# Normalised attention and leaky-ReLU MLP in one kernel: an opening in a new order, GpSimd squares behind gates, softmax sums by halves of the queries

## The chip, the cores and the metric

One core of one Trainium2 chip runs the whole program. The metric is the device time of one execution in microseconds; the median of three executions counts. Engine names are those of the profile: PE is TensorE's matmul side and PEld its weight load, DVE is VectorE, ACT is ScalarE, POOL is GpSimd, SP is SyncE.

## The reference

Queries, keys and values have 8 batches, 12 heads, 448 positions and 64 channels. Queries and keys are divided by their root mean square and scaled by a gain, then comes softmax attention, then a two-layer MLP on all heads of a position together (768 to 2048 to 768 channels, leaky ReLU between).

```python
def rmsnorm(x, g):
    rms = np.sqrt(np.mean(x * x, axis=-1, keepdims=True) + 1e-06)
    return x / rms * g
q_n, k_n = (rmsnorm(q, g_q), rmsnorm(k, g_k))
scores = scale * np.matmul(q_n, k_n.transpose(0, 1, 3, 2))
scores = scores - np.max(scores, axis=-1, keepdims=True)
attn = np.exp(scores)
attn = attn / (np.sum(attn, axis=-1, keepdims=True) + 1e-09)
attn_out = np.matmul(attn, v)
x = attn_out.transpose(0, 2, 1, 3).reshape(8 * 448, 768)
h = x @ w_in
out = np.maximum(0.01 * h, h) @ w_out
```

## The kernel before

The work is cut into 24 units of four heads of one batch; three units fill the 768 channels of a batch. A unit's q and k lie as 128 rows by 896 columns each. Per unit:

- squares (`prep_sq` on ACT or `prep_sqp` on GpSimd), their sums (`prep_ssq`, DVE), the inverse root (`prep_rinv`, two ACT instructions), the normalised values in fp16 (`prep_norm`, DVE), and a transposition, in the opening on PE;
- scores for seven groups of keys (`qk`), a shift from the maximum of the first group (`shift_max`, a broadcast by a matmul in `shift_mm`, and a bias `eb`), seven exponentials on ACT (`ex`);
- sums of the exponentials over the keys, by matmuls with ones, the product with v (`pv`), and a multiplication by the inverse sums (`xmul`).

The MLP's matmuls are held in a queue, and from unit 3 on they are dealt out between the steps of the attention. Units 0 to 2 have none of them beside them: this is the opening, written out by hand. `warm` issues matmuls whose results nobody uses. They keep TensorE active while there is no other work for it.

```python
            nc.scalar.activation(buf(u, f"sq{ti}")[:, :, c[0]:c[1]], raw[u][ti][:, :, c[0]:c[1]], AF.Square)

    def prep_sqp(u, tis=BOTH):
        for ti in tis:
            nc.gpsimd.tensor_tensor(buf(u, f"sq{ti}"), raw[u][ti], raw[u][ti], op=ALU.mult)

    def prep_g(u):
        nc.vector.tensor_scalar(buf(u, "qkT")[:, 0], buf(u, "qkT")[:, 0], gcol, None, op0=ALU.mult)

    def prep_ssq(u, c=ALL, tis=BOTH):
        for ti in tis:
            nc.vector.tensor_reduce(buf(u, "ssq")[:, ti, :, c[0]:c[1]], buf(u, f"sq{ti}")[:, :, c[0]:c[1]],
                                    axis=AXL.X, op=ALU.add)

    def prep_rinv(u, tis=BOTH):
        x = slice(tis[0], tis[-1] + 1)
        nc.scalar.activation(buf(u, "uu")[:, x], buf(u, "ssq")[:, x], AF.Ln, bias=eps_t, scale=1.0 / D)
        nc.scalar.activation(buf(u, "rinv")[:, x], buf(u, "uu")[:, x], AF.Exp, bias=0.0, scale=-0.5)

    def prep_norm(u, c=ALL, tis=BOTH):
        n = c[1] - c[0]
        for ti in tis:
            src = raw[u][ti]
            nc.vector.tensor_tensor(
                buf(u, "n16")[:, ti, c[0]:c[1]].rearrange("p s a d -> p a s d"), src[:, :, c[0]:c[1]],
                buf(u, "rinv")[:, ti, :, c[0]:c[1], None].broadcast_to([P, 2, n, D]), op=ALU.mult)

    def prep_tr(u, ti, copies):
        tp = aux([P, NS, P], FP16, "tp")
        for (lo, hi), copy in copies:
            for x in range(lo, hi):
...
    def shift_max(u):
        s = st[u]
        sT = s["sT"][0][1]
        if isinstance(sT, list):
            pm2 = small.tile([P, 2], FP32, tag="pm2", name="pm2")
            for a in range(2):
                nc.vector.tensor_reduce(pm2[:, a:a + 1], sT[a][:, 0:S], axis=AXL.X, op=ALU.max)
            s["spare"] = sT[0]
            nc.vector.tensor_reduce(s["spare"][:, 511:512], pm2, axis=AXL.X, op=ALU.max)
        else:
            s["spare"] = sT[:, 0]
            nc.vector.tensor_reduce(s["spare"][:, 511:512], sT[:, :, 0:S], axis=AXL.XY, op=ALU.max)
        s["dg"] = small.tile([P, P], FP16, tag="dg", name="dg")
        nc.vector.tensor_tensor(s["dg"], ident16, s["spare"][:, 511:512].broadcast_to([P, P]), op=ALU.mult)
...
    def shift_mm(u):
        s = st[u]
...
        else:
            if "pb" not in s:
                shift_bank(u)
            pb = s["pb"]
            nc.tensor.matmul(pb[:, 0:P], onesp, s["dg"], start=True, stop=True)
            nc.vector.tensor_reduce(s["spare"][:, 510:511], pb[:, 0:P], axis=AXL.X, op=ALU.max)
        s["eb"] = small.tile([P, 1], FP32, tag="eb", name="eb")
        nc.vector.tensor_scalar(s["eb"], s["spare"][:, 510:511], -1.0, DELTA, op0=ALU.mult, op1=ALU.add)

    def gate(u):
        nc.gpsimd.tensor_copy(gate_t, buf(u, "n16")[:, 1, NS - 1, 1, D - 1:D])
```

`gate` copies one element of the last normalised values on GpSimd. All that GpSimd does behind it, squares as well as its own transfers, therefore starts only when the normalisation has ended.

The sums for units 4 to 22 (`narrow`) use the column groups of TensorE: even groups of keys go to two of them, odd ones to the other two, and the two halves are added on DVE. Then ACT takes the logarithm and the exponential of its negative, and transfers spread the inverse sums over the rows.

```python
    def zcol(u):
        s = st[u]
        s["zc"] = aux([P, 512], FP32, "zc")
        for t in (0, 1, 6, 2, 3, 4, 5):
            for a in range(2):
                halves = ((t % 2, 0, S),) if t < NS - 1 else ((0, 0, S // 2), (1, S // 2, S))
                for y, lo, hi in halves:
                    c = 32 * (2 * y + a)
                    nc.tensor.matmul(s["zc"][c:c + 32, lo:hi], onesr, s["et"][:, t, a, lo:hi],
                                     start=(t < 2), stop=(t in (4, 5)))
...
    def zcol_sum(u):
        s = st[u]
        s["zs"] = zpool.tile([64, S], FP32, tag="zs", name="zs")
        nc.vector.tensor_copy(s["zs"], s["zc"][64:128, 0:S])
        nc.vector.tensor_tensor(s["zs"], s["zc"][0:64, 0:S], s["zs"], op=ALU.add)

    def zcol_inv(u):
        s = st[u]
        nc.scalar.activation(s["zs"], s["zs"], AF.Ln)
        nc.scalar.activation(s["zs"], s["zs"], AF.Exp, bias=0.0, scale=-1.0)
        s["rz"] = zpool.tile([P, 2, S], FP32, tag="rz", name="rz")
        for r in range(2):
            src = s["zs"][r:64:2, None, :]
            nc.sync.dma_start(s["rz"][:, r], src.broadcast_to([32, 4, S]))
```

The opening:

```python
        load(0)
        load(1)
        load(2)
        gps = aux([P, 512], FP32, "gps")
        wbank = aux([P, 512], FP32, "warm")
        warm(32, wbank)
        for a in range(2):
            nc.vector.scalar_tensor_tensor(gdup[:, a], grow[:, 0], 0.125, grow[:, 1], op0=ALU.mult, op1=ALU.mult)
        nc.tensor.matmul(gps[:, 0:1], gdup.rearrange("o a d -> o (a d)"), one32, start=True, stop=True)
        warm(42, wbank)
        prep_sq(0, CA, (0,))
        prep_sq(0, CB, (0,))
        prep_sq(0, ALL, (1,))
        prep_ssq(0, CA, (0,))
...
        nc.vector.tensor_copy(gcol, gps[:, 0:1])
        prep_ssq(0, ALL, (1,))
        prep_rinv(0, (1,))
        prep_sqp(1, (0,))
        load_v(0)
        load_v(1)
        prep_norm(0, CA, (0,))
        prep_norm(0, CB, (0,))
        prep_tr(0, 0, ((CA, acopy), (CB, acopy)))
        prep_norm(0, K0, (1,))
        tpk = aux([P, NS, P], FP16, "tp")

        def trk(c, copy):
            for x in range(*c):
                nc.tensor.transpose(tpk[:, x, :], buf(0, "n16")[:, 1, x].rearrange("p a d -> p (a d)"), ident16)
            copy(buf(0, "qkT")[:, 1, c[0]:c[1]], tpk[:, c[0]:c[1]])

        trk(K0, vcopy)
        prep_norm(0, K1, (1,))
        qk(0, STEPS[0])
        shift_max(0)
        trk(K1, acopy)
        load(3)
        prep_sqp(1, (1,))
        gate(0)
        load_w_in(0, 1024)
        prep_sqp(2)
        shift_bank(0)
        warm(12, st[0]["pb"])
        shift_mm(0)
        load_v(2)
        prep_ssq(1, ALL, (0,))

        def feed(u):
            load(u + 4)
            gate(u + 1)
            prep_sqp(u + 3)
            load_v(u + 3)
...
        def close(u):
            n = u + 1
            zsum_slot(u)
            ex(n)
            qk(n, (1,))
            pv(u)
            zinv(u)

        ex(0)
        prep_ssq(1, ALL, (1,))
        prep_rinv(1)
        prep_norm(1)
        prep_ssq(2)
        feed(0)
        load_w_in(1024, 1024)
        wb = aux([P, 512], FP32, "warm")
        qk(0, (1,))
        ex(0)
        warm(16, wb)
        qk(0, (2,))
        ex(0)
        warm(12, wb)
        qk(0, (3,))
        ex(0)
        warm(6, wb)
        qk(0, (4,))
        ex(0)
        trn(1, 0, vcopy)
        trn(1, 1, acopy)
        qk(0, (5,))
        ex(0)
        qk(0, (6,))
        ex(0)
        prep_rinv(2)
        score0(1)
        shift_max(1)
        shift_bank(1)
        warm(20, st[1]["pb"])
        shift_mm(1)
        close(0)
        ...
        prep_norm(2)
        prep_ssq(3)
        ex(1)
        feed(1)
        for f in range(2):
            load_w_out(8 * f, 8)
        qk(1, (2,))
```

The steps of a later unit that bear on the sums: `zcol` and `zcol_sum` run at the start of the next unit, `zcol_inv` in its first step, and the multiplication in the second step on GpSimd, or in the third on DVE for three of the units.

Of the kernel before, what the change touches and what calls it, by code (L numbers as in the profile page):

```python
# [18 lines left out]
def kernel(  # L19
# [113 lines left out]
# [3 lines that stand above are left out]
# [124 lines left out]

    def zcol(u):
        s = st[u]
        s["zc"] = aux([P, 512], FP32, "zc")
        for t in (0, 1, 6, 2, 3, 4, 5):
            for a in range(2):
                halves = ((t % 2, 0, S),) if t < NS - 1 else ((0, 0, S // 2), (1, S // 2, S))
                for y, lo, hi in halves:
                    c = 32 * (2 * y + a)
                    nc.tensor.matmul(s["zc"][c:c + 32, lo:hi], onesr, s["et"][:, t, a, lo:hi],  # L269
                                     start=(t < 2), stop=(t in (4, 5)))  # L270
# [12 lines left out]
    def zcol_sum(u):  # L283
        s = st[u]
        s["zs"] = zpool.tile([64, S], FP32, tag="zs", name="zs")
        nc.vector.tensor_copy(s["zs"], s["zc"][64:128, 0:S])
        nc.vector.tensor_tensor(s["zs"], s["zc"][0:64, 0:S], s["zs"], op=ALU.add)

    def zcol_inv(u):
        s = st[u]  # L290
        nc.scalar.activation(s["zs"], s["zs"], AF.Ln)
        nc.scalar.activation(s["zs"], s["zs"], AF.Exp, bias=0.0, scale=-1.0)  # L292
        s["rz"] = zpool.tile([P, 2, S], FP32, tag="rz", name="rz")
        for r in range(2):
            src = s["zs"][r:64:2, None, :]
            nc.sync.dma_start(s["rz"][:, r], src.broadcast_to([32, 4, S]))
# [279 lines left out]
    with tc.manual_schedule():  # L576
# [22 lines left out]
        prep_sqp(1, (0,))  # L599
        load_v(0)  # L600
        load_v(1)
        prep_norm(0, CA, (0,))
        prep_norm(0, CB, (0,))
        prep_tr(0, 0, ((CA, acopy), (CB, acopy)))
        prep_norm(0, K0, (1,))
        tpk = aux([P, NS, P], FP16, "tp")

        def trk(c, copy):
            for x in range(*c):
                nc.tensor.transpose(tpk[:, x, :], buf(0, "n16")[:, 1, x].rearrange("p a d -> p (a d)"), ident16)  # L610
            copy(buf(0, "qkT")[:, 1, c[0]:c[1]], tpk[:, c[0]:c[1]])

        trk(K0, vcopy)
        prep_norm(0, K1, (1,))
        qk(0, STEPS[0])
        shift_max(0)
        trk(K1, acopy)
        load(3)
        prep_sqp(1, (1,))
        gate(0)  # L620
        load_w_in(0, 1024)
        prep_sqp(2)
        shift_bank(0)
        warm(12, st[0]["pb"])
        shift_mm(0)
        load_v(2)
        prep_ssq(1, ALL, (0,))

        def feed(u):
            load(u + 4)  # L630
            gate(u + 1)
            prep_sqp(u + 3)
            load_v(u + 3)

        def trn(u, ti, copy):
            prep_tr(u, ti, ((ALL, copy),))
# [5 lines left out]
        def close(u):  # L642
            n = u + 1
            zsum_slot(u)
            ex(n)
            qk(n, (1,))
            pv(u)
            zinv(u)

        ex(0)  # L650
        prep_ssq(1, ALL, (1,))
        prep_rinv(1)
        prep_norm(1)
        prep_ssq(2)
        feed(0)
        load_w_in(1024, 1024)
        wb = aux([P, 512], FP32, "warm")
        qk(0, (1,))
        ex(0)
        warm(16, wb)  # L660
        qk(0, (2,))
        ex(0)
        warm(12, wb)
        qk(0, (3,))
        ex(0)
        warm(6, wb)
        qk(0, (4,))
        ex(0)
        trn(1, 0, vcopy)
        trn(1, 1, acopy)  # L670
        qk(0, (5,))
        ex(0)
        qk(0, (6,))
        ex(0)
        prep_rinv(2)
# [3 lines left out]
        warm(20, st[1]["pb"])  # L679
        shift_mm(1)  # L680
        close(0)

        prep_norm(2)
        prep_ssq(3)
        ex(1)
        feed(1)
# [13 lines left out]
        prep_rinv(3)  # L700
# [7 lines left out]
        close(1)  # L708

        prep_norm(3)  # L710
        ex(2)
        feed(2)
# [137 lines left out]
```

## Time and profile before

| quantity | value |
|---|---|
| median of three executions | 431.97 us (430.81 to 432.87) |
| profiled execution, span | 429.5 us |
| mean granted TensorE clock | 0.992 |
| unused matmuls (`warm`) | 152 |
| first exponential of unit 0 | starts at 17.67 us |
| first exponential of unit 1 | starts at 28.48 us |
| first exponential of unit 2 | starts at 37.40 us |
| first exponential of unit 3 | starts at 49.60 us |

The profile gives busy time by engine, by stretch of the span, by group of like instructions, and the instructions in order of time. Bracketed entries tell how long the engine was idle ahead of an instruction and what ended that. A busy matmul engine is not necessarily one at its peak, because a matmul's recorded length holds its pipeline as well. A long duration of a DVE or GpSimd instruction need not be work: an engine that has begun an instruction and cannot go on is recorded as busy.

### The profile page before, as it was taken

What the parts mean: (1) busy time and instruction counts of PE and PEld (TensorE: products, weight loads), DVE (VectorE), ACT (ScalarE), POOL (GpSimd) and SP (SyncE); (2) the same over time, 40 slices, a digit from 0 to 9 for tenths busy, and PEclk for the clock granted to TensorE, in tenths of its full rate; (3) what the DMA queues carried; (4) which work ended last, traced back from release to release, by engine and by line L of the source; (5) the groups of instructions that cost most, each with busy time, mean ns of one, the idle gap of its engine ahead of it and who ended that gap; (6) DMA issues with size and microseconds to landing.
All of it is one profiled execution on the core that took longest, in us unless ns stands there. A gap on an engine that the chain in (4) does not pass through costs nothing.

```text
span 429.5 us, 8844 instructions
## 1 busy us (share of the span) xinstructions
PE 409.5 (95%) x3645; PEld 211.3 (49%) x3645; DVE 272.1 (63%) x434; ACT 306.5 (71%) x466; POOL 86.5 (20%) x77
## 2 busy tenths in 40 slices
PE   7677999999999999999999999999999999999996
PEld 6444444444444544455445544455445544455563
DVE  5898656888669865487359864587459840541162
ACT  4389888757986779967986789967986767643400
POOL 3875323300002102111102102111101101110000
PEclk9699999999999999999999999999999999999999
DMA  7999994789666896578665797489582460212013
GB/s 253 196 241 249 240 248 110 120 183 221 168 104 115 190 215 161 140 133 195 170 111 130 188 192 168 134 140 188 169 110 44 118 149 11 44 38 73 2 45 103
DMA packets 66476, 62.37 MB, mean 145 GB/s; under 512 B 35716, under 2 KB 61572, under 8 KB 66436
## 3 DMA queue, kind: packets, MB, share of 16 engines
q1 hardware_dynamic: 55840, 49.62, 47.0%
q0 software_dynamic: 10272, 11.80, 17.9%
q8 instruction: 28, 0.46, 0.4%
q10 hardware_dynamic: 324, 0.39, 0.3%
q14 instruction: 12, 0.10, 0.1%
HBM read 45.61 MB, written 11.01 MB: 132 GB/s over the span
## 4 chain that ended last, share of the span: by engine, by line
PE 64%; ACT 17%; DVE 10%; issue 2%; DMA 1%; SPq 0%; ACTq 0%; DVEq 0%
PE hps L347 23%; ACT et L201 8%; PE md L427 7%; PE mc L427 7%; PE sT L182 6%; PE ma L427 6%; PE sT L326 5%; ACT gt L341 4%; PE op L387 3%; PE zc L269 3%; PE mb L427 2%; DVE n L154 2%; ACT x L281 1%; DVE ssq L142 1%; ACT zs L292 1%
## 5 line engine op out<-in xcount | busy, mean ns | idle before, releaser
L201 ACT ACTIVATE et<-sT,eb 128x896 f16<-128x896 f32 x166 | 158.5, 1004 | 15.6 <-PE sT L182 13.3
L347 PE MATMUL hps<-xt,win 128*128 128x448 f16 x756 | 151.1, 353 | 0.2 <-DVE xt L335 0.2
L347 PEld LDWEIGHTS <-win 128*128 128x128 f16 x756 | 70.6, 98 | 71.5 <-issue 10.1
L341 ACT ACTIVATE gt<-hps 128x448 f16<-128x448 f32 x126 | 65.7, 540 | 19.3 <-PE hps L347 18.7
L306 POOL TENSOR_TENSOR xt<-x,rz 128x896 f16<-128x896 f32 x16 | 33.5, 2091 | 150.1 <-DMA rz<-zs 49.1
L154 DVE TENSOR_TENSOR n<-rq,rinv 128x896 f16<-128x896 f32 (+2 forms) x25 | 29.0, 1164 | 47.8 <-ACT rinv L148 44.3
L182 PE MATMUL sT<-qkT 64*64 64x448 f16 x664 | 52.8, 367 | 4.7 <-ACT et L201 4.2
L142 DVE TENSOR_REDUCE ssq<-sq 128x14 f32<-128x896 f32 (+2 forms) x49 | 50.3, 1055 | 1.3 <-ACT sq L131 1.3
L427 PEld LDWEIGHTS <-sa 128*128 128x128 f16 x352 | 32.8, 98 | 26.3 <-issue 6.1
L281 ACT COPY x<-sT 128x896 f32<-128x896 f32 x19 | 17.2, 906 | 37.8 <-DVE sT L232 37.8
L111 POOL DMA_DIRECT2D vt<-in_v_dram x24 | 18.2, 758 | 112.2 <-PE sT L326 104.8
L219 DVE TENSOR_REDUCE sT<-sT 128x1 f32<-128x896 f32 x22 | 24.0, 1093 | 18.3 <-PE sT L182 18.3
L182 PEld LDWEIGHTS <-qkT 64*64 64x64 f16 x672 | 15.8, 104 | 38.9 <-issue 35.5
L427 PEld LDWEIGHTS <-gt 128*128 128x128 f16 x264 | 25.3, 98 | 19.0 <-issue 2.9
L387 PE MATMUL op<-wout,gt 128*128 128x384 f16 x192 | 34.1, 327 | 0.0
L427 PE MATMUL ma<-wout,gt 128*128 128x384 f16 x176 | 32.3, 326 | 0.4
L154 DVE TENSOR_TENSOR n<-rk,rinv 128x896 f16<-128x896 f32 (+2 forms) x25 | 28.9, 1156 | 0.0
L326 PE MATMUL sT<-et,vt 64*64 64x448 f16 x532 | 28.5, 349 | 0.3
L408 DVE TENSOR_TENSOR sa<-gt 128x512 f16<-128x512 f16 (+1 forms) x15 | 8.1, 542 | 30.3 <-ACT gt L341 30.3
L326 PEld LDWEIGHTS <-vt 64*64 64x64 f16 x672 | 20.4, 107 | 10.8 <-issue 1.1
L387 PEld LDWEIGHTS <-gt 128*128 128x128 f16 x192 | 17.7, 98 | 14.0 <-issue 3.2
L453 ACT COPY ost<-ma 128x384 f32<-128x384 f32 x11 | 5.3, 479 | 23.7 <-PE ma L427 23.7
(87 smaller groups left out, 443.5 us busy)
## 6 DMA issues: line engine op xcount, KB each, us to landing
rq<-in_q_dram SPq DMA_DIRECT2D x24, 448.0 KB, 4.8
rk<-in_k_dram SPq DMA_DIRECT2D x24, 448.0 KB, 5.9
out_dram<-ost SPq DMA_DIRECT2D x52, 192.0 KB, 4.0
rz<-zs SPq DMA_DIRECT2D x38, 224.0 KB, 3.3
vt<-in_v_dram POOLq DMA_DIRECT2D x24, 224.0 KB, 5.0
win<-in_moe_w_in_dram POOLq DMA_DIRECT2D x8, 384.0 KB, 8.9
wout<-in_moe_w_out_dram POOLq DMA_DIRECT2D x2, 1536.0 KB, 23.7
out_dram<-ost SPq DMA_DIRECT2D x4, 96.0 KB, 2.1
```

What stands on the lines that cost most here:

```text
L142: nc.vector.tensor_reduce(buf(u, "ssq")[:, ti, :, c[0]:c[1]], buf(u, f"sq{ti}")[:, :, c[0]:c[1]], axis=AXL.X, op=ALU.add)
L154: nc.vector.tensor_tensor(buf(u, "n16")[:, ti, c[0]:c[1]].rearrange("p s a d -> p a s d"), src[:, :, c[0]:c[1]], buf(u, "rinv")[:, ti, :, ...
L182: nc.tensor.matmul(banks[a][64 * r:64 * r + 64, 0:S].rearrange("p (t x) -> p t x", t=NS), kT(u, r, a, t), qT(u, r, a), start=True, stop=True)
L201: nc.scalar.activation(s["et"][:, t], sT[:, :, 0:S], AF.Exp, bias=s["eb"], scale=1.0)
L219: nc.vector.tensor_reduce(s["spare"][:, 511:512], sT[:, :, 0:S], axis=AXL.XY, op=ALU.max)
L281: nc.scalar.copy(s["x32"], s["pslot"][:, :, 0:S])
L306: eng.tensor_tensor(xts[b][:, g], s["x32"], s["rz"], op=ALU.mult)
L326: nc.tensor.matmul(s["pv"][r][64 * a:64 * a + 64, 0:S], vts[u % NV][64 * r:64 * r + 64, a, t], s["et"][64 * r:64 * r + 64, t, a], start=(t ...
L341: nc.scalar.activation(dst, src, AF.Prelu, bias=0.0, scale=1.0, alpha=0.01)
L347: nc.tensor.matmul(hps[:, 0:S], win16[:, kt // 2, kt % 2, ts(ft, P)], xt[:, kt // 2, kt % 2], start=(kt == 0), stop=(kt == KT - 1))
L387: nc.tensor.matmul(op2[:, 0:HC], gt[:, ft, ds(col(t), P)], wout16[:, ft, ds(HC * half, HC)], start=(ft == 0), stop=(ft == FT - 1))
L427: nc.tensor.matmul(bank[:, 0:HC], a[:, f], b[:, f], start=(first and f == 0), stop=(f == HF - 1), skip_group_check=not first)
```

## The change

It has two parts. The first sets the opening in a new order. The squares of unit 1 go from GpSimd to ACT. GpSimd's squares of units 2 to 5 and its transfers of v and of the weights stand behind the gate of a unit, so that they do not run beside that unit's normalisation. All four pieces of unit 0's normalisation follow each other on DVE. The inverse roots of unit 1 are taken for q and k apart. The scores and the shift of unit 1 come before the last two groups of unit 0, and the sums of squares of units 2 and 3 move behind the shift of the unit ahead. The blocks of unused matmuls behind the two leading ones change from 12, 16, 12, 6 and 20 to 6, 12, 8, 10 and 8.

The second part splits the softmax sums by halves of the queries, not by even and odd groups of keys. A matmul takes one half of the queries of two groups of keys at once, and one reduction on DVE adds the two. The sums then lie on 128 rows of 224 columns and no longer on 64 rows of 448, for the two ACT instructions too; four transfers of half rows take the place of two.

```diff
--- before.py
+++ after.py
@@ -258,16 +258,17 @@
         s["zt"] = [s["zslot"][:, r] for r in range(2)]
         zsum(u)
 
+    HS = S // 2
+
     def zcol(u):
         s = st[u]
         s["zc"] = aux([P, 512], FP32, "zc")
-        for t in (0, 1, 6, 2, 3, 4, 5):
-            for a in range(2):
-                halves = ((t % 2, 0, S),) if t < NS - 1 else ((0, 0, S // 2), (1, S // 2, S))
-                for y, lo, hi in halves:
+        for i, (t, n) in enumerate(((0, 2), (NS - 1, 1), (2, 2), (4, 2))):
+            for y in range(2):
+                for a in range(2):
                     c = 32 * (2 * y + a)
-                    nc.tensor.matmul(s["zc"][c:c + 32, lo:hi], onesr, s["et"][:, t, a, lo:hi],
-                                     start=(t < 2), stop=(t in (4, 5)))
+                    nc.tensor.matmul(s["zc"][c:c + 32, 0:n * HS].rearrange("p (k x) -> p k x", k=n), onesr,
+                                     s["et"][:, t:t + n, a, HS * y:HS * y + HS], start=(i == 0), stop=(i == 3))
 
     def pv_slot(u):
         s = st[u]
@@ -282,9 +283,8 @@
 
     def zcol_sum(u):
         s = st[u]
-        s["zs"] = zpool.tile([64, S], FP32, tag="zs", name="zs")
-        nc.vector.tensor_copy(s["zs"], s["zc"][64:128, 0:S])
-        nc.vector.tensor_tensor(s["zs"], s["zc"][0:64, 0:S], s["zs"], op=ALU.add)
+        s["zs"] = zpool.tile([P, HS], FP32, tag="zs", name="zs")
+        nc.vector.tensor_reduce(s["zs"], s["zc"][:, 0:S].rearrange("p (k x) -> p x k", k=2), axis=AXL.X, op=ALU.add)
 
     def zcol_inv(u):
         s = st[u]
@@ -292,8 +292,9 @@
         nc.scalar.activation(s["zs"], s["zs"], AF.Exp, bias=0.0, scale=-1.0)
         s["rz"] = zpool.tile([P, 2, S], FP32, tag="rz", name="rz")
         for r in range(2):
-            src = s["zs"][r:64:2, None, :]
-            nc.sync.dma_start(s["rz"][:, r], src.broadcast_to([32, 4, S]))
+            for y in range(2):
+                src = s["zs"][64 * y + r:64 * y + 64:2, None, :]
+                nc.sync.dma_start(s["rz"][:, r, HS * y:HS * y + HS], src.broadcast_to([32, 4, HS]))
 
     def xmul_sb(u):
         xmul_pool(u, nc.vector)
@@ -596,41 +597,39 @@
         nc.vector.tensor_copy(gcol, gps[:, 0:1])
         prep_ssq(0, ALL, (1,))
         prep_rinv(0, (1,))
-        prep_sqp(1, (0,))
-        load_v(0)
-        load_v(1)
         prep_norm(0, CA, (0,))
         prep_norm(0, CB, (0,))
-        prep_tr(0, 0, ((CA, acopy), (CB, acopy)))
         prep_norm(0, K0, (1,))
-        tpk = aux([P, NS, P], FP16, "tp")
-
-        def trk(c, copy):
-            for x in range(*c):
-                nc.tensor.transpose(tpk[:, x, :], buf(0, "n16")[:, 1, x].rearrange("p a d -> p (a d)"), ident16)
-            copy(buf(0, "qkT")[:, 1, c[0]:c[1]], tpk[:, c[0]:c[1]])
-
-        trk(K0, vcopy)
         prep_norm(0, K1, (1,))
+
+        def tr(u, ti, chunks, tp=None):
+            if tp is None:
+                tp = aux([P, NS, P], FP16, "tp")
+            for c, copy in chunks:
+                for x in range(*c):
+                    nc.tensor.transpose(tp[:, x, :], buf(u, "n16")[:, ti, x].rearrange("p a d -> p (a d)"), ident16)
+                copy(buf(u, "qkT")[:, ti, c[0]:c[1]], tp[:, c[0]:c[1]], ti == 0)
+            return tp
+
+        tr(0, 0, ((CA, acopy),))
+        tr(0, 0, ((CB, acopy),))
+        tpk = tr(0, 1, ((K0, vcopy),))
+        prep_sq(1, ALL, (0,))
         qk(0, STEPS[0])
         shift_max(0)
-        trk(K1, acopy)
+        tr(0, 1, ((K1, acopy),), tpk)
+        prep_sq(1, ALL, (1,))
         load(3)
-        prep_sqp(1, (1,))
         gate(0)
+        load_v(0)
+        prep_sqp(2, (0,))
         load_w_in(0, 1024)
-        prep_sqp(2)
+        load_v(1)
+        load_v(2)
         shift_bank(0)
-        warm(12, st[0]["pb"])
+        warm(6, st[0]["pb"])
         shift_mm(0)
-        load_v(2)
-        prep_ssq(1, ALL, (0,))
-
-        def feed(u):
-            load(u + 4)
-            gate(u + 1)
-            prep_sqp(u + 3)
-            load_v(u + 3)
+        prep_ssq(1)
 
         def trn(u, ti, copy):
             prep_tr(u, ti, ((ALL, copy),))
@@ -639,51 +638,55 @@
             zsum(u, t0, t1)
             pv(u, t0, t1)
 
-        def close(u):
-            n = u + 1
-            zsum_slot(u)
-            ex(n)
-            qk(n, (1,))
-            pv(u)
-            zinv(u)
-
         ex(0)
-        prep_ssq(1, ALL, (1,))
-        prep_rinv(1)
-        prep_norm(1)
-        prep_ssq(2)
-        feed(0)
+        prep_rinv(1, (0,))
+        qk(0, (1,))
+        ex(0)
+        prep_rinv(1, (1,))
+        prep_norm(1, ALL, (0,))
+        prep_norm(1, K0, (1,))
+        prep_norm(1, K1, (1,))
+        load(4)
+        gate(1)
+        prep_sqp(2, (1,))
         load_w_in(1024, 1024)
         wb = aux([P, 512], FP32, "warm")
-        qk(0, (1,))
-        ex(0)
-        warm(16, wb)
+        warm(12, wb)
         qk(0, (2,))
         ex(0)
-        warm(12, wb)
+        warm(8, wb)
         qk(0, (3,))
+        tr(1, 0, ((ALL, acopy),))
+        tpk = tr(1, 1, ((K0, vcopy),))
         ex(0)
-        warm(6, wb)
         qk(0, (4,))
         ex(0)
-        trn(1, 0, vcopy)
-        trn(1, 1, acopy)
-        qk(0, (5,))
-        ex(0)
-        qk(0, (6,))
-        ex(0)
-        prep_rinv(2)
+        tr(1, 1, ((K1, vcopy),), tpk)
         score0(1)
         shift_max(1)
         shift_bank(1)
-        warm(20, st[1]["pb"])
+        warm(10, st[1]["pb"])
+        qk(0, (5,))
+        ex(0)
+        warm(8, st[1]["pb"])
+        qk(0, (6,))
+        ex(0)
         shift_mm(1)
-        close(0)
-
+        prep_ssq(2)
+        ex(1)
+        qk(1, (1,))
+        ex(1)
+        zsum_slot(0)
+        pv(0)
+        prep_rinv(2)
+        zinv(0)
         prep_norm(2)
-        prep_ssq(3)
-        ex(1)
-        feed(1)
+        gate(2)
+        prep_sqp(3)
+        load_v(3)
+        load(5)
+        prep_sqp(4, (0,))
+        load_v(4)
         for f in range(2):
             load_w_out(8 * f, 8)
         qk(1, (2,))
@@ -697,7 +700,6 @@
         ex(1)
         qk(1, (5,))
         ex(1)
-        prep_rinv(3)
         score0(2)
         shift_max(2)
         qk(1, (6,))
@@ -705,11 +707,21 @@
         shift_bank(2)
         warm(12, st[2]["pb"])
         shift_mm(2)
-        close(1)
+        prep_ssq(3)
+        ex(2)
+        qk(2, (1,))
+        ex(2)
+        zsum_slot(1)
+        pv(1)
+        prep_rinv(3)
+        zinv(1)
 
         prep_norm(3)
-        ex(2)
-        feed(2)
+        load(6)
+        gate(3)
+        prep_sqp(4, (1,))
+        prep_sqp(5)
+        load_v(5)
         qk(2, (2,))
         ex(2)
         trn(3, 0, vcopy)
```

## Prediction

> **What bounds the kernel now.** I read the page first (busy shares, slices), then busy time by stretch, since one average would mix an opening without MoE work with a long stretch that has it. Columns: stretch; PE, PEld, DVE, ACT, POOL busy us with instruction counts; granted clock; DMA share; GB/s.
>
> ```profile
> PE 409.5 (95%) x3645; PEld 211.3 (49%) x3645; DVE 272.1 (63%) x434; ACT 306.5 (71%) x466; POOL 86.5 (20%) x77
> ...
> 12.00:18.00 6.00, 3.92 (x33) 2.76 (x34) 4.63 (x8) 1.13 (x2) 4.34 (x7) 0.64 1.01 231
> ...
> 30.00:36.00 6.00, 4.26 (x69) 2.56 (x62) 5.71 (x9) 5.97 (x8) 5.43 (x6) 1.00 1.14 237
> 36.00:42.00 6.00, 4.88 (x88) 2.90 (x86) 4.47 (x10) 5.82 (x9) 2.34 (x3) 1.00 1.13 246
> ...
> 156.00:172.00 16.00, 16.00 (x137) 7.51 (x135) 9.09 (x14) 15.54 (x27) 2.83 (x2) 1.00 0.78 180
> ```
>
> From about 60 us to the end PE is busy 15 to 16 of every 16 us: PE sets the time there. From 28 to 48 us ACT is full (5.97 and 5.82 of 6) and DVE nearly so: the exponentials of units 0 to 2 run with too little matmul beside them. Before 18 us no engine is full, so dependencies set the time. I next read the opening in order of time (start, duration, engine, line).
>
> ```profile
> 7.79 2.63 DVE L154 TENSOR_TENSOR n<-rq,rinv 128x512 f16<-128x512 f32 x2
> 8.21 1.80 POOL L135 TENSOR_TENSOR sq<-rq 128x896 f32<-128x896 f32 x1 [6.90 <-DMA rq<-in_q_dram]
> 10.34 3.08 DVE L154 TENSOR_TENSOR n<-rk,rinv 128x128 f16<-128x128 f32 x1
> 11.57 1.69 POOL L135 TENSOR_TENSOR sq<-rk 128x896 f32<-128x896 f32 x1
> 13.89 0.95 DVE L154 TENSOR_TENSOR n<-rk,rinv 128x768 f16<-128x768 f32 x1
> 17.67 1.01 ACT L201 ACTIVATE et<-sT,eb 128x896 f16<-128x896 f32 x1 [1.12 <-DVE eb L240]
> ...
> 28.48 1.16 ACT L199 ACTIVATE et<-s,eb 128x448 f16<-128x448 f32 x2 [1.59 <-DVE eb L240]
> ```
>
> A normalisation of 128 columns takes 3.08 us, one of 768 columns 0.95: the short one stands beside GpSimd's squares of unit 1 (8.21 to 13.26). The first exponential waits for this until 17.67, the first of unit 1 until 28.48. Finally the forms of the softmax sums:
>
> ```profile
> L286 DVE COPY zs<-zc 64x448 f32<-64x448 f32 x19 | 11.9, 626 | 0.6
> L287 DVE TENSOR_TENSOR zs<-zc,zs 64x448 f32<-64x448 f32 x19 | 11.7, 617 | 0.6
> L292 ACT ACTIVATE zs<-zs 64x448 f32<-64x448 f32 x19 | 11.0, 577 | 0.6
> L291 ACT ACTIVATE zs<-zs 64x448 f32<-64x448 f32 x19 | 10.8, 568 | 0.0
> L214 DVE TENSOR_REDUCE pm<-s 128x1 f32<-128x448 f32 x4 | 2.3, 614 | 0.5 <-PE s L182 0.5
> ```
>
> **What the Trainium skill says.** "SBUF — State Buffer", section "Who interferes with whom": a VectorE instruction with two SBUF inputs contends with a GpSimd instruction that reads SBUF, and the first to start keeps the other out for its whole length; reductions never contend. The trace agrees in both: the 3.08 us above, and two sums of squares at 17.55 that keep 1.03 us each beside a GpSimd square at 17.58. The same section infers that descriptor generation needs only the write side; here the blocked 128-column piece also overlaps two descriptor writes (9.95 to 11.55), so the trace leaves that unsettled. "TensorE: Matmul & The Clock Gate", "What's actually happening": an idle array falls to half clock. The trace agrees: PE has long gaps between 8.9 and 14.0, and the grant is 0.64 from 12 to 18. "DMA: Bandwidth & Descriptors", "Specifications": pieces of 512 B or more run at line rate; the halved rows here become 896 B, and no run yet shows that size.
>
> **The change, part one: up to the first exponential.** GpSimd's squares of unit 1 (two of about 1.7 us) go to ACT, which is idle between 8.45 and 17.67 but for three copies; two of 0.95 there. The v loads move behind a gate. So unit 0's normalisations run unblocked: 0.68 for 512 columns (measured), 0.55 for 384 and 0.27 for 128 (on the line through 0.68 and 0.95, 1.05 ns a column), 0.95 for 768. DVE starts at 7.79 and ends at 10.2, not 14.8. The copy of the first K tile now stands behind all four: about 10.4 on DVE. Scores end by 11.0, the maximum (1.09) and the diagonal (0.29) by 12.4, the broadcast (0.25), its reduction (0.30) and the bias (0.16) by about 13.2. ACT: copies to 10.2, square of q to 11.2, copy of K (0.80) to 12.5, square of k to 13.4. Its data is there: q and k of unit 1 landed 6.4 and 7.2 us after issue at 1.76 and 2.28, hence at 8.2 and 9.5. First exponential: 13.4 in place of 17.67, **4.3 us** earlier.
>
> **Part two: up to unit 1.** Unit 0 needs seven exponentials (1.0, then about 0.92 each: 6.5), two split pairs for the inverse root (0.5 each), one 0.92 copy: 8.4, so 13.4 + 8.4 = 21.8. Unit 1's scores now come before the last two exponentials, not behind them. DVE: sums for unit 1 to 15.3, normalisation (2.3) to 17.7, copies to 19, maximum and diagonal (1.7) to 20.7, bias at 21.5. It is ready in time, so the holes that ACT now has at 18.68 (0.98) and before 28.48 (1.59) close. Unit 1 starts at 21.8 in place of 28.48: **6.6 us**.
>
> **Part three: units 1 and 2.** Here some is lost again. Unit 1 on ACT: 1.16 + 6 x 0.91 + root 0.55 + sum inverse 1.87 = 9.0, so 30.9. DVE is later: root ready at 24.5, then normalisation 2.2 to 26.7, waits and copies of the transposes 1.3, multiplication by the inverse sums 1.15, scores 0.4, maximum to diagonal 1.7, broadcast to bias 0.8: 24.5 + 7.6 = 32.1. Unit 2 starts at 32.1, against 37.40: **5.3 us**. In unit 2 the root of unit 3 is added (0.55; previously in unit 1) and the sums of unit 3 (2.07) now stand in front of it. From the start of unit 2 to the end of its inverse sums was 48.51 - 37.40 = 11.1; I add 0.55 and a wait of 0.3: 44.1 in place of 48.5, **4.4 us** at the hand-over to steady work. The unused matmuls behind the two leading blocks fall from 66 to 44. At about 0.08 us each that is 1.8 us of PE time, off the path, because PE is busy 4.3 to 4.9 of 6 there.
>
> **Part four: softmax sums in 19 units.** The matmuls stay 12 of 448 and 4 of 224 columns per unit on four column groups: no PE gain. DVE: 0.626 + 0.617 becomes one reduction of 448 columns, 0.614 by the row above: 0.63 saved per unit, 12 us in all. ACT: 128x448 takes 540 ns and 128x896 1004, so 1.04 ns a column; 224 columns fewer make both 0.23 shorter: 0.46 per unit, 8.7 us in all. But SyncE issues four transfers of about 0.59 instead of two, so the last part leaves about 1.2 later; that cancels the 1.1 saved ahead of it. Most of this lies beside a full PE. PE's missing busy time in the windows from 60 to 364 sums to 3.4 us; I credit **0.5 us**.
>
> Sum: 4.4 + 0.5 = 4.9; 431.97 - 4.9 = 427.1, taken as **427.0 us**.
>
> **Rivals.** (1) The transfers take the place of ACT. DMA share is above 1.0 from 12 to 60 us, and starting loads earlier creates no bandwidth. For it: the second half of w_out lands 28.4 us after its issue at 35.6, v of unit 5 20.9 after. Against it: weights of the first layer land by about 27.5 and 42 (issue 16.9 + 10.7, 29.0 + 12.9), and the first half, the only one needed for the first matmuls, is issued about 2 us earlier. If a load is late: gain 1 to 2, 430 us. (2) DVE limits more than I take. It has about 28 us of work between the first bias at 13.2 and 44; if descriptor writes of GpSimd block the normalisation of unit 1 (up to 1.4 us), or the moved sums (2.07 each) hold up the roots, the gain is 2.5 to 3.5: 429 us. (3) The opening is fully ACT-bound: 5.6 at the hand-over (no DVE loss of 1.2), and the relief on DVE and ACT closes half of the 3.4: 424.7. (4) The four transfers delay the multiplication, and with it the first layer: the chain of waits holds one such transfer (3.74 us at 82.25). If it costs 0.1 a unit, 2 us of the gain go: 429.
>
> **Range and chances.** Most terms are measured durations; the uncertainty is in their order. 424.3 to 430.2 holds rivals 2 to 4 and nearly rival 1. Two per cent faster would be 423.3, beyond even rival 3: 0.06. Two per cent slower would be 440.6; that needs a new wait in every unit: 0.02. The rest, 0.92, within.
>
> **What will show it.** Right: unit 0's normalisations near 0.2 to 0.95 each; first exponential near 13.4; unit 1 near 21.8, unit 2 near 32; no MoE wait on w_in; the sums' reduction near 0.6 and both activations near 0.34; PE windows after 60 us as full as now. Wrong: a normalisation of unit 1 above 1.5 us beside descriptor writes; squares on ACT waiting for DMA; ACT idle ahead of units 1 or 2 by more than 1.5; a hand-over before 44 that is not seen at the end (then the MoE stretch was not PE-bound); POOL or DVE waits on rz growing.

## Result and profile after

The changed kernel takes 424.39 us (median of 4, 424.36 to 425.58) against 431.43 us of the kernel before (430.81 to 432.87): ratio 0.984, 95% interval 0.981 to 0.987. That is 7.0 us, where the sum of the prediction was 4.9. The time lies within the predicted 424.3 to 430.2 us, but close to its lower end.

The busy line of the page, then busy time by stretch (columns as in the prediction; the last stretch has the same length and lies 5 us earlier, as the work in it does):

```profile
PE 407.0 (96%) x3623; PEld 207.3 (49%) x3623; DVE 256.2 (61%) x417; ACT 302.9 (72%) x470; POOL 83.3 (20%) x75
...
12.00:18.00 6.00, 6.00 (x54) 3.73 (x50) 4.71 (x8) 5.16 (x10) 5.50 (x9) 0.50 1.08 206
...
30.00:36.00 6.00, 4.41 (x83) 2.79 (x86) 5.18 (x8) 5.18 (x8) 4.88 (x7) 1.00 1.11 261
36.00:42.00 6.00, 5.34 (x80) 2.59 (x75) 5.01 (x7) 5.17 (x8) 5.23 (x4) 1.00 1.14 258
...
151.00:167.00 16.00, 16.00 (x139) 7.40 (x142) 7.87 (x12) 15.22 (x28) 2.83 (x2) 1.00 0.80 180
```

ACT works from 12 us on (5.16 of 6, before 1.13). From 30 to 42 us it is no longer full (5.18 and 5.17, before 5.97 and 5.82): holes have opened there. The TensorE clock is at one half from 12 to 18 us, and PE looks full there because each matmul takes longer.

The opening in order of time:

```profile
7.23 1.15 DVE L154 TENSOR_TENSOR n<-rq,rinv 128x512 f16<-128x512 f32 x2
8.29 1.15 DVE L154 TENSOR_TENSOR n<-rk,rinv 128x128 f16<-128x128 f32 x2
9.45 0.95 ACT L131 ACTIVATE sq<-rq 128x896 f32<-128x896 f32 x1
12.16 2.54 POOL L90 DMA_DIRECT2D win<-in_moe_w_in_dram  x4
12.45 1.01 ACT L201 ACTIVATE et<-sT,eb 128x896 f16<-128x896 f32 x1 [0.30 <-DVE eb L240]
14.32 1.08 DVE L154 TENSOR_TENSOR n<-rq,rinv 128x896 f16<-128x896 f32 x1
14.69 1.47 POOL L111 DMA_DIRECT2D vt<-in_v_dram  x2
21.18 1.17 ACT L199 ACTIVATE et<-s,eb 128x448 f16<-128x448 f32 x2
30.60 1.16 ACT L199 ACTIVATE et<-s,eb 128x448 f16<-128x448 f32 x2 [0.62 <-DVE eb L240]
```

Unit 0's four normalisation pieces take 1.15 and 1.15 us together, where one alone took 3.08. The first exponential comes at 12.45, those of units 1 and 2 at 21.18 and 30.60. The normalisation at 14.32 keeps 1.08 us, although GpSimd writes descriptors beside it, for w_in until 14.70 and for v from 14.69. In e5 below the same happens at 18.32, again with 1.08 us. So what the prediction left open is settled here: these descriptor writes did not hold up the normalisation.

The groups of the softmax sums:

```profile
L287 DVE TENSOR_REDUCE zs<-zc 128x224 f32<-128x448 f32 x19 | 11.8, 623 | 0.6 <-issue 0.4
L291 ACT ACTIVATE zs<-zs 128x224 f32<-128x224 f32 x19 | 7.5, 395 | 0.0
L292 ACT ACTIVATE zs<-zs 128x224 f32<-128x224 f32 x19 | 7.4, 390 | 0.6
```

One reduction of 0.623 us stands for two DVE instructions. The ACT pair takes 0.785 us in place of 1.145: 0.36 saved per unit.

To compare kernels I use three marks of each trace: the first exponential; the load of v issued in unit 3 ("hand-over"), shortly after the first MLP matmuls; and the load of v issued in unit 20 ("late"). "Way" is hand-over minus first exponential; "stretch" is late minus hand-over. The clock is the grant from 12 to 15 and from 15 to 18 us. Each row is one profiled execution, and two things vary between executions without any edit: when k of unit 0 lands (the sums of its squares start between 6.21 and 7.06 us in the fourteen traces, 6.78 before and 6.22 changed), and when the full clock returns.

| kernel | first exp. | unit 1 | hand-over | way | stretch | clock |
|---|---|---|---|---|---|---|
| before | 17.67 | 28.48 | 52.23 | 34.56 | 261.57 | 0.78, 0.50 |
| changed | 12.45 | 21.18 | 46.93 | 34.48 | 260.02 | 0.50, 0.51 |
| e1 opening only | 12.46 | 20.59 | 46.38 | 33.92 | 261.53 | 0.50, 1.00 |
| e2 sums only | 14.03 | 27.94 | 52.40 | 38.37 | 260.01 | 0.50, 0.93 |
| e3 unit 1's squares on ACT | 13.00 | 24.41 | 49.29 | 36.29 | 261.50 | 1.00, 1.00 |
| e4 v behind the gate | 15.50 | 28.27 | 53.04 | 37.54 | 261.57 | 0.50, 0.51 |
| e5 squares back on GpSimd | 16.45 | 25.16 | 50.93 | 34.48 | 260.05 | 0.50, 0.50 |
| e6 few unused matmuls | 13.17 | 21.62 | 47.94 | 34.77 | 260.22 | 0.50, 0.50 |
| e7 DVE time back | 12.87 | 21.00 | 46.77 | 33.90 | 260.21 | 1.00, 1.00 |
| e8 ACT time back | 12.48 | 20.62 | 46.39 | 33.91 | 261.96 | 0.50, 0.99 |
| e9 ACT time behind | 12.39 | 20.54 | 46.30 | 33.91 | 267.05 | 0.50, 0.93 |
| e10 moves | 12.54 | 21.33 | 46.13 | 33.59 | 260.02 | 0.50, 0.50 |
| e11 more unused matmuls | 13.01 | 21.13 | 46.91 | 33.90 | 260.38 | 1.00, 1.00 |
| e12 both | 12.81 | 20.93 | 46.04 | 33.23 | 260.02 | 1.00, 1.00 |

Between before and changed, 5.30 us are gained by the hand-over and 1.55 in the stretch: 6.85 of the 6.9 between the spans (429.5 and 422.6). The clock has its share in the way of the new opening: 33.90 to 33.92 where the full clock is there from about 15 us on (e1, e7, e8, e9, e11), 34.48 where the half clock lasts to 18 (changed, e5).

### The profile page after: what moved, and what is told of

Same layout as the page of the kernel before. It is cut to its first block, busy times and chain, and to the rows that moved or that the text cites. A ratio compares the mean times of both kernels' runs of the same rounds, so it can differ in the third digit from the quotient of the medians.

```text
span 422.6 us, 8871 instructions
## 1 busy us (share of the span) xinstructions
PE 407.0 (96%) x3623; PEld 207.3 (49%) x3623; DVE 256.2 (61%) x417; ACT 302.9 (72%) x470; POOL 83.3 (20%) x75
## 4 chain that ended last, share of the span: by engine, by line
PE 83%; DVE 8%; ACT 6%; issue 1%; DMA 1%; SPq 0%; DVEq 0%
PE hps L348 34%; PE sT L182 8%; PE ma L428 7%; PE md L428 7%; PE mc L428 7%; PE sT L327 6%; PE op L388 4%; ACT et L201 4%; PE mb L428 3%; PE zc L270 3%; DVE n L154 2%; DVE ssq L142 1%; DMA rk<-in_k_dram 1%; PE pv L327 1%; DVE xt L336 1%
## 5 line engine op out<-in xcount | busy, mean ns | idle before, releaser
L307 POOL TENSOR_TENSOR xt<-x,rz 128x896 f16<-128x896 f32 x16 | 33.7, 2104 | 145.5 <-DMA rz<-zs 114.7
L154 DVE TENSOR_TENSOR n<-rq,rinv 128x896 f16<-128x896 f32 (+2 forms) x25 | 27.1, 1086 | 50.8 <-ACT rinv L148 47.7
L111 POOL DMA_DIRECT2D vt<-in_v_dram x24 | 18.2, 757 | 114.7 <-PE sT L327 107.2
L154 DVE TENSOR_TENSOR n<-rk,rinv 128x896 f16<-128x896 f32 (+2 forms) x26 | 26.1, 1010 | 0.0
## 6 DMA issues: line engine op xcount, KB each, us to landing
win<-in_moe_w_in_dram POOLq DMA_DIRECT2D x8, 384.0 KB, 12.6
```

What stands on the lines that cost most here:

```text
L111: nc.gpsimd.dma_start(vts[u % NV].rearrange("p a t d -> p a (t d)"), rows(v, u))
L154: nc.vector.tensor_tensor(buf(u, "n16")[:, ti, c[0]:c[1]].rearrange("p s a d -> p a s d"), src[:, :, c[0]:c[1]], buf(u, "rinv")[:, ti, :, ...
L307: eng.tensor_tensor(xts[b][:, g], s["x32"], s["rz"], op=ALU.mult)
```

## Experiments

**The two parts alone.** e1 is the changed kernel with the old sums, e2 the kernel before with the new sums.

```diff
# e1, against the changed kernel: zcol, zcol_sum and zcol_inv as before
-        s["zs"] = zpool.tile([P, HS], FP32, tag="zs", name="zs")
-        nc.vector.tensor_reduce(s["zs"], ...)
+        s["zs"] = zpool.tile([64, S], FP32, tag="zs", name="zs")
+        nc.vector.tensor_copy(s["zs"], s["zc"][64:128, 0:S])
+        nc.vector.tensor_tensor(s["zs"], s["zc"][0:64, 0:S], s["zs"], op=ALU.add)
...
# e2, against the kernel before: the three functions as changed, the opening untouched
```

Expected of e1:

> The new opening with the old softmax sums. Theory (the opening brings about 5.3 us, the sums the other 1.5 to 1.7): ratio 0.987 to 0.989, about 426 us; first matmuls of the first MLP layer for unit 3 start about 5.3 us earlier than in the kernel before, and that lead neither grows nor shrinks afterwards. Rival (the opening brings all of it and the lead grows on its own): ratio 0.984, 424.5 us, the lead grows to 7 us although the sums are the old ones.

Expected of e2:

> The old opening with the new softmax sums. Theory: 1.3 to 1.8 us faster than before, ratio 0.996 to 0.997; the opening up to the first exponential of unit 3 (49.6 us) is unchanged and the lead builds up in steps over units 5 to 22. Rival (the sums are hidden behind a full TensorE, as in most windows): ratio 0.999 to 1.000. Second rival (four transfers in place of two cost something): slower.

e1: 425.48 us, ratio 0.9865 (0.985 to 0.988), by the ratio 5.8 us below the kernel before, which took 431.39 beside it. Its lead at the hand-over is 5.85, more than the 5.30 of the changed kernel, which goes with its full clock coming back sooner, and the stretch is the old one. e2: 429.81 us, ratio 0.9966 (0.9953 to 0.9979), by the ratio 1.5 us below; stretch 260.01. The product 0.983 agrees with the whole change. So the parts add, and the sums are worth 1.5; they are not hidden behind a full TensorE, as the rival for e2 had it.

**What held up unit 0's normalisation.** e3 takes only the squares of unit 1 off GpSimd; e4 leaves them and moves only the loads of v.

```diff
# e3, against the kernel before
-        prep_sqp(1, (0,))
...
         trk(K0, vcopy)
+        prep_sq(1, ALL, (0,))
...
         trk(K1, acopy)
+        prep_sq(1, ALL, (1,))
...
-        prep_sqp(1, (1,))
# e4, against the kernel before
-        load_v(0)
-        load_v(1)
...
         gate(0)
+        load_v(0)
+        load_v(1)
```

Expected of e3:

> The kernel before with one thing changed: both squares of unit 1 on ACT, v loads and all else where they were. Theory (GpSimd's reads hold up unit 0's normalisation): the 128-column normalisation falls from 3.08 to about 0.3 us, the first exponential comes 4 to 5 us earlier (12.5 to 13.5), and about 3 of that are left at unit 1, whose chain of sums, root and normalisation is otherwise as before; ratio 0.993 to 0.995. Rival (descriptor writes for v hold it up): the normalisation stays above 1.5 us long and the first exponential gains under 2 us.

Expected of e4:

> The kernel before with the loads of v for units 0 and 1 moved behind the gate, the squares of unit 1 still on GpSimd. Theory (squares alone hold up the normalisation): the two squares follow each other from 8.2 to 11.6, the normalisations of unit 0 are held until about 11.7, so the first exponential comes about 1.6 us earlier, by the 1.6 us that the descriptors took between the squares; ratio 0.997 to 0.999. Rival (descriptor writes hold it up): normalisations of 0.3 to 1 us from 10 on, and the first exponential 3 to 4 us earlier.

e3: 428.30 us, ratio 0.9925 (0.9909 to 0.9942). The 128-column piece takes 0.28 us and the first exponential comes at 13.00. But with the squares gone, GpSimd writes the first two loads of v at 1.27 and 2.49 us, long before the pieces. So e3 alone does not tell squares from descriptors; e4 and, below, e5 do. e4: 431.72 us, ratio 1.0007 (0.9997 to 1.0017). Its opening in order of time:

```profile
8.28 1.89 POOL L135 TENSOR_TENSOR sq<-rq 128x896 f32<-128x896 f32 x1 [6.97 <-DMA rq<-in_q_dram]
8.55 1.77 DVE L154 TENSOR_TENSOR n<-rk,rinv 128x128 f16<-128x128 f32 x1
10.13 1.72 POOL L135 TENSOR_TENSOR sq<-rk 128x896 f32<-128x896 f32 x1
10.78 1.89 DVE L154 TENSOR_TENSOR n<-rk,rinv 128x768 f16<-128x768 f32 x1
...
18.15 1.45 DVE L154 TENSOR_TENSOR n<-rq,rinv 128x896 f16<-128x896 f32 x1 [0.70 <-issue]
18.59 2.54 POOL L135 TENSOR_TENSOR sq<-rk 128x896 f32<-128x896 f32 x1
19.52 2.56 DVE L154 TENSOR_TENSOR n<-rk,rinv 128x896 f16<-128x896 f32 x1
```

The squares alone suffice to hold up the pieces, with no descriptor written beside them. What I had not expected is how little of the earlier start is left. e4 starts its exponentials 2.2 us earlier (0.3 of it a sooner landing of k) and hands over 0.8 later. e2 teaches the same by chance: with the old opening, q of unit 1 landed a little later, a piece slipped ahead of the square (first exponential 14.03), and nothing of it is left at the hand-over either. The second half of the fence shows why. Unit 1's normalisation, now earlier, meets GpSimd's squares of unit 2: two pieces of 1.08 become 1.45 and 2.56 (in e2 2.57 and 2.56), and the square itself is held, 2.54 for 1.69. In the kernel before, the late start had spared unit 1 most of this collision (1.54 and 1.08). A cost removed at one place came back at the next. e3 keeps 3.1 us because GpSimd, rid of two squares, is nearly done with unit 2's when unit 1 comes (2.08 and 1.08). The remaining 2.6 us between e3 and e1 (by their ratios) belong to the gates and the new order together; they were not separated.

e5 undoes the squares alone in the new order:

```diff
# e5, against the changed kernel
         prep_rinv(0, (1,))
+        prep_sqp(1)
...
-        prep_sq(1, ALL, (0,))
-        prep_sq(1, ALL, (1,))
```

> The changed kernel with one thing undone: both squares of unit 1 back on GpSimd, ahead of the gate, at the old place. Theory (they hold up unit 0's normalisation): normalisations of unit 0 end near 11.7 instead of 9.4, first exponential near 14.7 instead of 12.4, hand-over 2 to 2.5 us later than in the changed kernel, ratio to the kernel before 0.988 to 0.990. Rival (what counts is the order of unit 1 alone, as the early first exponentials that brought nothing in the old order suggest): the hand-over is at most 0.7 us later, ratio 0.984 to 0.986.

428.11 us, ratio 0.9931 (0.9913 to 0.995): by the ratios 4.0 us are lost, more than either guess. The two K pieces took 1.15 us together in the changed kernel. Here they stand beside GpSimd's squares (8.94 to 12.43):

```profile
9.13 4.12 DVE L154 TENSOR_TENSOR n<-rk,rinv 128x128 f16<-128x128 f32 x2
```

The first exponential moves to 16.45, 4.0 us later, of which 0.84 is a later landing of k in that execution (the sums of its squares start at 7.06, not 6.22). The way is 34.48, that of the changed kernel at the same clock. In the new order, which has a gate ahead of the next squares, delay at the start passes on in full.

**The unused matmuls.** The chain of waits of the changed kernel, in order of time, holds two blocks that the prediction had put beside the path:

```profile
12.40 1.40 PE warm L575 x12
13.80 0.52 PE sT L182 x4
14.31 0.97 PE warm L575 x8
```

At half clock a matmul of 128 columns takes 0.12 us, and the scores have to wait for them.

```diff
# e6, against the changed kernel
-        warm(6, st[0]["pb"])
...
-        warm(12, wb)
+        warm(1, wb)
...
-        warm(8, wb)
...
-        warm(10, st[1]["pb"])
...
-        warm(8, st[1]["pb"])
# e11, against the changed kernel
         tpk = tr(0, 1, ((K0, vcopy),))
+        warm(8, wbank)
...
-        warm(6, st[0]["pb"])
+        warm(14, st[0]["pb"])
```

Expected of e6:

> The changed kernel without the unused matmuls of unit 0's and unit 1's groups (44 become 1; the two leading blocks and the last 12 stay). Theory (while the clock is at one half, the blocks of 12 and 8 stand on the chain to unit 1): unit 1 starts 0.3 to 0.7 us earlier than in the profile of the changed kernel, 20.5 to 20.9, ratio 0.9825 to 0.984. Rival (they keep the clock up): a clock of one half lasts past 18 us, transposes and scores of unit 1 take 0.6 us and more, unit 1 starts later than 21.2. Second rival (off the path): no change of unit 1 by more than 0.2.

Expected of e11:

> The changed kernel with 8 unused matmuls more ahead of the first scores and 14 instead of 6 ahead of the first shift, both where TensorE waits. Theory (the half clock from 12 to 18 us comes from gaps of TensorE between 7 and 12; with full clock the way from the first exponential to the hand-over is 27.4 us and not 28.0): clock 1.0 throughout 12 to 18, hand-over 0.3 to 0.6 us earlier, ratio 0.982 to 0.984. Rival (the additional matmuls stand in the way themselves or the grant falls anyway): no gain, 0.984 to 0.986.

e6: 425.66 us, ratio 0.987 (0.9852 to 0.9888), about 1.3 slower than the changed kernel; the intervals overlap, and in its profile k landed 0.7 later, so the size is not certain. Unit 1 comes 8.45 us after the first exponential, not 8.73, so the blocks did stand in the way. But the clock now stays down much longer:

```profile
18.00:21.00 3.00, 2.41 (x22) 0.80 (x20) 2.13 (x5) 3.00 (x5) 3.00 (x4) 0.50 1.10 225
21.00:24.00 3.00, 2.76 (x29) 1.49 (x32) 2.45 (x4) 2.97 (x6) 0.72 (x2) 0.50 1.10 252
```

Unit 0's sums over the keys then take 2.83 us for 28 matmuls instead of 1.52, and the way grows from 34.48 to 34.77. Both theories hold a part: the blocks cost at half clock, and without them the full clock comes back later. The grants, as means over each of the four executions, agree: 0.984 to 0.988 in e6, 0.990 to 0.995 in the changed kernel.

e11: full clock throughout, and a way of 33.90, 0.58 shorter than the changed kernel's. Yet 424.85 us, ratio 0.986 (0.9846 to 0.9875): no gain in the time. In the profile, its unit 0 started 0.6 later, because k landed 0.6 later (6.84 for 6.22), not because of the additional matmuls. And e1, e8 and e9 have the same way without them. Full clock from 12 us on also came once without the additional matmuls (e7), and in the other seven kernels with the new order it did not. So two for two (e11, e12) hints at a cause but does not show it.

**Which engine the sums relieve.** e7 gives DVE its old time back, e8 ACT. In both, the added instruction's result is not used.

```diff
# e7, against the changed kernel
         s["zs"] = zpool.tile([P, HS], FP32, tag="zs", name="zs")
+        zdum = zpool.tile([64, S], FP16, tag="zdum", name="zdum")
+        nc.vector.tensor_copy(zdum, s["zc"][64:128, 0:S])
# e8, against the changed kernel
+        zdum = zpool.tile([P, HS], FP32, tag="zdum", name="zdum")
+        nc.scalar.activation(zdum, s["zs"], AF.Ln)
         nc.scalar.activation(s["zs"], s["zs"], AF.Ln)
```

Expected of e7:

> The changed kernel with a copy of 64 x 448 on DVE put ahead of the reduction in each of the 19 units; its result is not used, and DVE's time is that of the old sums again. Theory (TensorE's waits for the diagonal of the maximum fell with DVE's load): those waits go back from 1.0 us to about 1.5, 0.4 to 0.9 us of the sums' 1.5 are lost, ratio 0.985 to 0.987. Rival (ACT's relief alone brought the gain): no change against the changed kernel.

Expected of e8:

> The changed kernel with a third ACT instruction of 128 x 224 ahead of the two in each of the 19 units (about 0.39 us; result unused), which gives ACT its old time for the sums. Theory (part of the gain is that TensorE waits less for exponentials to free a score bank): those waits go from 0.4 back to about 1 us, 0.4 to 0.9 us are lost, ratio 0.985 to 0.987. Rival (DVE's relief alone): no change against the changed kernel.

e7: 424.06 us, ratio 0.9838 (0.9822 to 0.9853), stretch 260.21: giving DVE its 12 us back costs at most 0.2. e8: 426.38 us, ratio 0.9901 (0.9879 to 0.9922), stretch 261.96: all of the sums' gain is gone and 0.4 more. So it is ACT's side that can lose the gain. TensorE's waits after 55 us, of the kernel before, of the changed kernel and then of e8:

```profile
PE sT L231 <- DVE dg L221: 1.5, 4, 0.8
PE sT L182 <- ACT et L201: 1.3, 4, 0.4
```

```profile
PE sT L231 <- DVE dg L221: 1.0, 1, 1.0
PE sT L182 <- ACT et L201: 0.4, 1, 0.4
```

```profile
PE sT L231 <- DVE dg L221: 1.0, 2, 0.7
PE sT L182 <- ACT et L201: 1.0, 3, 0.4
PE ma L430 <- DVE ost L446: 0.5, 3, 0.2
```

The wait of scores for an exponential to free their bank goes from 0.4 to 1.0 us, three times instead of once. The wait for the diagonal of the maximum, 1.5 with the old sums, stays at 1.0 in e8 and in e7. So neither engine's time alone brings that part back, and the rows above account for 1.1 of the 1.9 us that e8's stretch loses.

e8 delays the inverse sums as well as using ACT time. e9 puts the same instruction behind the transfers:

```diff
# e9, against the changed kernel, at the end of zcol_inv
+        zdum = zpool.tile([P, HS], FP32, tag="zdum", name="zdum")
+        nc.scalar.activation(zdum, s["zs"], AF.Exp, bias=0.0, scale=-1.0)
```

> The changed kernel with the third ACT instruction of 128 x 224 (about 0.39 us, result unused) behind the transfers of the inverse sums instead of ahead of the two that make them: the same ACT time as in the run before it, but the sums are on their way as early as in the changed kernel. Theory (ACT's busy time counts: exponentials come later and hold TensorE's score banks): nearly all of the loss stays, ratio 0.988 to 0.991, stretch from the loads of v in unit 3 to those in unit 20 near 261.5 to 262. Rival (the later inverse sums counted): the loss goes, ratio 0.983 to 0.985, stretch near 260.0.

It came out otherwise: 433.94 us, ratio 1.0061 (1.0037 to 1.0084), slower than the kernel before. The trace shows why:

```profile
123.69 2.06 POOL L309 TENSOR_TENSOR xt<-x,rz 128x896 f16<-128x896 f32 x1 [8.00 <-DMA rz<-zs]
123.71 2.33 DVE L414 TENSOR_TENSOR sa<-sa,gt 128x512 f16<-128x512 f16 x1
...
126.10 0.82 PE L430 MATMUL mb<-tw,sa 128*128 128x384 f16 x4 [1.30 <-DVE sa L414]
```

DVE's work for the second layer waits for an ACT result, and its subtraction comes 8.73 us after the last load of v ahead of it, 0.75 later than in the changed kernel (7.98). GpSimd's multiplication, which there starts 0.36 us behind the subtraction, now starts 0.02 us ahead of it and holds it for 2.33 us instead of 0.43; TensorE waits for the result. TensorE has such waits for this operand three times, 3.8 us in all, and between the two loads of v around the first of them pass 20.78 us instead of 16.58.

So e9 doesn't answer its question as a whole. One part of its trace is free of these waits, between the loads of v in units 9 and 14: 79.27 us in e9, 78.97 in the changed kernel, e2 and e7, 79.29 in e1, 79.37 in e8. The sums are alike, but it is not the same loss. With the old sums, 0.27 of it falls between the loads of units 12 and 13 (16.39 us in e1, 16.12 changed), next to a TensorE wait of 0.23 for the diagonal of the maximum. There e8 loses 0.14 and e9 0.05, and neither has that wait. Between the loads of units 10 and 11, and 11 and 12, it is the reverse: e8 and e9 lose 0.12 to 0.14 each time, the old sums at most 0.04. Added ACT time does cost something, then, but that it was busy time which made the old sums slower, and not the later inverse sums or both with DVE's part, is not shown.

**A better order?** ACT's holes in the profile after suggest three moves:

```diff
# e10, against the changed kernel
         tpk = tr(1, 1, ((K0, vcopy),))
+        prep_ssq(2, ALL, (0,))
...
-        prep_ssq(2)
+        prep_ssq(2, ALL, (1,))
...
         trn(3, 0, vcopy)
+        qk(2, (3,))
+        ex(2)
         trn(3, 1, vcopy)
...
-        qk(2, (3,))
-        ex(2)
...
-        sums(2, 0, 3)
         qk(2, (5,))
         ex(2)
-        sums(2, 3, 4)
+        zsum(2, 0, 3)
         qk(2, (6,))
         ex(2)
+        pv(2, 0, 3)
+        sums(2, 3, 4)
# e12: e10 and e11 together
```

Expected of e10:

> The changed kernel with three moves in the opening: the sums of squares for q of unit 2 go into a gap of DVE ahead of unit 1's shift; scores of group 3 of unit 2 come ahead of the second transposition of unit 3; scores of groups 5 and 6 of unit 2 come ahead of the sums over the keys. Theory (ACT idles 0.62 ahead of unit 2, 0.43 and 0.49 within it, for scores or a bias): those three holes close, the hand-over comes 1.0 to 1.6 us earlier after the same first exponential, ratio 0.980 to 0.982. Rival (DVE takes the place of TensorE as what ACT waits for): under 0.5 us, ratio 0.983 to 0.985.

Expected of e12:

> Both together: the three moves and the additional unused matmuls. If both theories hold they add: 1.3 to 2.2 us below the changed kernel, ratio 0.979 to 0.981. If only the moves hold: 0.980 to 0.982.

e10: 424.31 us, ratio 0.9846 (0.9827 to 0.9865). In its trace the way is 33.59, 0.9 shorter at the same clock, and groups 2 to 6 of unit 2 follow each other without a hole. The first move did nothing: unit 2 comes 18.19 us after the first exponential (18.15 before the move), as the inverse root stands behind two exponentials on ACT anyway. e12: 423.53 us, ratio 0.983 (0.9813 to 0.9847), way 33.23. The traces show about 1.2 us less of way, some 0.6 of it with the full clock and 0.7 with the moves (33.90 in e11), but the intervals of e10, e12 and the changed kernel overlap; no version is shown to beat the change.

## Why the prediction was right, and where not

**The number.** The gain came out 2.1 us above the sum, and 424.39 us is barely above the lower end of the range, 424.3. About half of the 2.1 is a mis-sized term (part four), and 0.56 is chance, as far as the profiles show. That the time still fell within the range is in part luck.

**Part one** (4.3 us up to the first exponential): the mechanism holds, shown by e3, e4 and e5. Measured 5.2, of which 0.56 is an earlier start of the squared sums of k (6.22 for 6.78), because k of unit 0 landed sooner in that execution (chance, as the spread from 6.21 to 7.06 shows).

**Part two** (6.6): 7.3 measured, 6.7 without the landing. The prediction took for granted that an earlier first exponential is an earlier unit 1. e2 and e4 show that it need not be: in the old order their gain was lost to the next collision, whereas in the new order it passes on in full (e5). Whether the gate alone does this was not tested; e3 kept 3.1 us without it, with fewer squares on GpSimd. The profile of before did not show that collision at its full size, because its late start evaded it.

**Part three** (5.3, then 4.4): 6.8 and 5.3 measured, 6.2 and 4.7 without the landing. Two errors cancelled. DVE's chain from the root of unit 2 to the bias took 6.9, not 7.6 (23.71 to 30.57). And from the start of unit 2 to the end of its inverse sums it is 12.6 us (30.60 to 43.23), not 12.0, for these waits in the changed kernel:

```profile
36.27 1.90 ACT L201 ACTIVATE et<-sT,eb 128x896 f16<-128x896 f32 x2 [0.43 <-PE sT L182]
38.67 1.90 ACT L201 ACTIVATE et<-sT,eb 128x896 f16<-128x896 f32 x2 [0.49 <-PE sT L182]
```

The scores stand behind a transposition and behind sums on TensorE, as e10 confirms. I had looked for such waits on DVE.

The step "off the path, because PE is busy 4.3 to 4.9 of 6 there" failed: unused matmuls were on the chain to unit 1 at half clock, and without them the full clock returned later (e6).

**Part four** is the mis-sized term: 0.5 credited, 1.5 measured (e2), about half of the 2.1 by which the sum was short. The step that failed is that most of the relief lies beside a full TensorE. It held for DVE's 12 us, worth at most 0.2 by themselves (e7), and not for ACT's side, where e8 loses the whole gain. The saving on ACT itself is smaller than I worked out: 0.36 per unit, because I took 1.04 ns a column from two different forms. The Trainium skill, "ScalarE: Activation LUTs", "What ACT_TABLE_LOAD costs", gives 186 ns + 0.833 ns a column for immediate scale and bias, 373 ns at 224 columns by that estimate; the trace has 390 and 395, against my 340.

**Rivals.** Late transfers (1) did not appear: the DMA share stays above 1.0, but no TensorE wait for weights shows. DVE as the limit (2) did not appear beyond the chain of part three; the descriptor writes hold nothing up. Rival (3) has the nearest number, 424.7, and its terms, 5.6 at the hand-over and half of 3.4 behind it, are near the measured 5.3 and 1.55. Its reasons hold only in part: 0.56 of the 5.3 is chance, the opening is not fully ACT-bound (the waits above, and 0.62 ahead of unit 2), and DVE's relief alone is not what counts. The four transfers (4): GpSimd's waits for the inverse sums grew from 49.1 to 114.7 us, which the prediction had named as a sign of being wrong. But the multiplication's idle time for all reasons together fell, from 150.1 to 145.5 us; what grew is the part for which the inverse sums were the last to come. They land in 2.3 instead of 3.3 us, and the stretch is shorter, not longer.

## What to carry to other kernels

When GpSimd and VectorE (POOL and DVE in the profile) both do elementwise work on two operands from SBUF, look for every place where they can meet, not only the one in the profile: removing one delay moves the next instruction into the next collision, and here the gain lasted in an order with a gate on GpSimd's work. Engine time that is freed counts only if the engine releases something the bounding engine waits for; here 0.36 us per unit on ACT's side counted, and 0.62 us of DVE by itself did not. Test it by giving the time back to one engine at a time, and compare the traces stretch by stretch: an added instruction also brings losses of its own (e9).

## What the runs showed of the hardware

- The blocking goes both ways: a GpSimd square of 1.69 us took 2.54 beside a VectorE normalisation (e4), and a 512-column fp16 subtraction of 0.43 took 2.33 when GpSimd began 0.02 us earlier (e9).
- A normalisation with two SBUF inputs kept its 1.08 us beside GpSimd's descriptor writes (changed kernel, 14.32; e5, 18.32).
- With unused matmuls taken out, the clock stayed at one half from 12 to 24 us although PE was recorded busy 1.6 to 2.8 of every 3 us (e6).
- In the same opening, a half clock that lasted from 12 to 18 us, and not to about 15 or less, went with a way longer by 0.6 us (34.48 for 33.90 to 33.92).
